# Issuing stores of token rows and routing weights, and the first loads of v, from other DMA queues

## The chip, the cores and the metric

The kernel runs on one core of a Trainium2 chip. Its engines are TensorE (PE, with its weight loads PEld), VectorE (DVE), ScalarE (ACT), GpSimd (POOL) and SyncE (SP). A DMA is started by an instruction in the queue of SP, ACT or POOL; the data are then moved by the core's 16 DMA engines. The metric is the device time of one execution in microseconds, as the median of several runs.

## The reference

Three layers follow each other on 4 x 576 = 2304 tokens of 512 values:

```python
scores = scale * q @ k.T + alibi_bias        # 4 batches, 8 heads, causal, window 128
x = softmax(scores) @ v                      # rows of 8 heads x 64
x = (silu(x @ w_gate) * (x @ w_val)) @ w_out # 512 -> 1536 -> 512
logits = x @ g_w + log1p(exp(x @ n_w)) * noise
out[token] = sum over its top 2 of 8 experts: weight * relu(x @ w1[e]) @ w2[e]
```

## The kernel before, in words

**Attention.** Heads go in pairs: a batch b has four pairs p. `load_qk` and `load_v` (lines 178 and 183) load a pair's q, k and v through `load_nat` (line 120), which starts three DMAs per tensor: one for each head's first 512 rows (line 124, 128 KB each) and one for the last 64 rows of both heads (line 125, 32 KB). Line 122 picks the queue: k of the very first pair goes by ACT, v of batch 0's first two pairs by POOL, all else by SP. At the start of the program the calls stand in this order (lines 191 to 195): q and k of pair 0, q and k of pair 1, v of pair 0, v of pair 1. The q, k and v of pairs 2 and 3 are loaded when an earlier pair has freed the buffer (line 535).

**First dense layer.** Its weights come in pieces of 512 KB. In batch group 0 each piece is loaded raw into `cs` by SP (`Convert.load`, line 221), rearranged by ACT (lines 246 and 247) and DVE (248 and 249) into `wst`, stored to a scratch tensor (line 250), and split into a high and a low part, `wu`, by ACT (line 295) and DVE (line 296). For later groups SP loads the scratch pieces into `wst` (line 279, three buffers) and ACT and POOL do the split. Each matmul is done as three (`three`, lines 321 to 323). The attention of group b+1 is interleaved with the dense layer of group b.

**Rows.** At the end of each group, `yo` (line 625) copies finished rows of 128 tokens from the accumulators to `X2` (tile xT), by ACT (line 644) or DVE (line 642), and stores each 128 x 512 block into the DRAM tensor `x2d` (line 646, POOL, 18 stores of 256 KB in all). A row of `x2d` has 520 values: 512 of the token, 8 routing weights.

**Routing and experts.** `route` is called twice, for the first three groups (13 blocks of tokens) and for the last one (5 blocks). Its `weigh` (line 770) computes the weights `wd` on ACT and DVE and stores them into the last 8 columns of `x2d` (line 782, POOL, two stores). From the chosen slots `decode` makes index lists, and `gather` (line 904) has POOL fetch expert rows from `x2d` by an indirect DMA. The expert weights w1, w2 pass through the same `wst` buffers (line 279, SP) and the same split.

**Order of work.** SP, ACT and POOL each work through one queue in order, DMA instructions included. Which instruction comes when is written by hand for DVE and POOL in the first stretch (to line 1007) and for PE in one stretch near the end (line 1063); elsewhere a scheduler orders each queue when the program is built, by playing the program through a timing simulation (`schedule_with_timeline_sim=True`, line 1164).

Of the kernel before, what the change touches and what calls it, by code (L numbers as in the profile page):

```python
# [24 lines left out]
def f32(ap):  # L25
    return ap.bitcast(F32)
# [3 lines left out]
def tile_alibi_window_attention__swiglu__noisy_top2_moe(  # L30
# [15 lines left out]
    nc = tc.nc  # L46
    B, H, S, D = q.shape
    DM = H * D
# [13 lines left out]
    TP = 128  # L62
# [6 lines left out]
    RW = DM + E  # L69
# [8 lines left out]
    def bank(i):  # L78
        return psum.tile([128, 512], F32, name=f"b{i}", tag=f"b{i}")

    x2d = dram.tile([NT, RW], F32, name="x2d")
# [37 lines left out]

    def load_nat(t, src, b, p, rest=None):  # L120

        eng = nc.scalar if src is k and (b, p) == (0, 0) else nc.gpsimd if src is v and b == 0 and p < 2 else nc.sync
        for i in range(2):
            eng.dma_start(t[:, 0:4, i, :], src[b, 2 * p + i, 0:512, :].rearrange("(i p) d -> p i d", p=128))
        eng.dma_start(t[0:64, 4] if rest is None else rest, src[b, 2 * p:2 * p + 2, 512:576, :].rearrange("h p d -> p h d"))
        return t
# [51 lines left out]
    def load_qk(b, p):  # L178
        qn, kn = (buffers(b, p).nat(x) for x in ("qn", "kn"))
        NAT[b, p, "q"] = load_nat(qn, q, b, p)  # L180
        NAT[b, p, "k"] = load_nat(kn, k, b, p, qn[64:128, 4])

    def load_v(b, p):
        bf = buffers(b, p)
        NAT[b, p, "i"] = bf.nv % 2
        bf.nv += 1
        load_nat(bf.v[NAT[b, p, "i"]], v, b, p)
# [131 lines left out]
    def three(ps, st, mv, first, last):  # L319

        nc.tensor.matmul(ps, st(0), mv(0), start=first, stop=False, skip_group_check=True)  # L321
        nc.tensor.matmul(ps, st(0), mv(1), start=False, stop=False, skip_group_check=True)  # L322
        nc.tensor.matmul(ps, st(1), mv(0), start=False, stop=last, skip_group_check=True)  # L323
# [4 lines left out]
    def new_xt(i, dt=F32R):  # L328
        return main.tile([128, 2, KC * GW], dt, name=f"xT{i % 2}")
# [4 lines left out]
    def xt_part(b, s):  # L334
        return XT[b][:, s, :].rearrange("p (c s) -> p c s", c=KC)

    def blocks(b):
        return GRP[b][1] // 128
# [235 lines left out]
    def gbank(b):  # L574
        gcount[0] += 1
        l = (0, 1, 2) if b < B - 1 else (0, 1, 2, 4, 5)
        return bank(l[gcount[0] % len(l)])

    def mlp1(b):

        base = b * UB
        n = GRP[b][1]
        cut = (0, n) if n <= 512 else (0, n // 2, n)

        def hh(s, f, sl):
            t, f = (HT[0], f) if f < NFA else (HT[1], f - NFA)
            return t[:, s, f * GW + sl.start:f * GW + sl.stop]

        def gv(f):
            st = {}  # L590

            def go(which, half, cs):
                def run():
                    u = base + 2 * f + which
                    sl = slice(cut[half], cut[half + 1])
                    w_ = sl.stop - sl.start
                    if cs.start == 0:
                        if half == 0:
                            ws.split(u + 3)
                        st["ps", which, half] = gbank(b)  # L600
                    w, ps = ws.tile[u], st["ps", which, half]
                    for c in range(cs.start, cs.stop):
                        three(ps[:, :w_], lambda s: w[:, s, c * 128:(c + 1) * 128],
                              lambda s: xt_part(b, s)[:, c, sl], c == 0, c == KC - 1)
                    if cs.stop < KC:
                        return
                    if which == 0:
                        t = wpool[1].tile([128, HW], F32, name="sg", bufs=3)[:, :w_]
                        nc.scalar.activation(t, ps[:, :w_], AF.Tanh, scale=0.5)
                        nc.vector.scalar_tensor_tensor(t, t, 1.0, ps[:, :w_], op0=OP.add, op1=OP.mult)  # L610
                        st["t", half] = t
                    else:
                        t = st["t", half]
                        nc.vector.scalar_tensor_tensor(t, t, 0.5, ps[:, :w_], op0=OP.mult, op1=OP.mult)
                        nc.scalar.activation(hh(0, f, sl), t, AF.Copy)  # L615
                        nc.vector.tensor_sub(hh(1, f, sl), t, f32(hh(0, f, sl)))  # L616
                return run
            parts = [slice(0, KC)] if len(cut) > 2 else [slice(0, 2), slice(2, KC)]
            return [go(w, h, cs) for w in range(2) for h in range(len(cut) - 1) for cs in parts]

        hidden = []
        for f in range(NF):
            hidden += gv(f)

        def yo(f, half):
            def run():
                u = base + 2 * NF + f
                if half == 0:
                    ws.split(u + 3)
                w = ws.tile[u]  # L630
                if f == 0 and half == 0:
                    std.l = dict(std.yo[blocks(b)])
                    YB1[b] = [bank(i) for i in range(blocks(b))]
                for i in range(2) if half == 0 else range(2, blocks(b)):
                    ps = YB1[b][i]
                    three(ps, lambda s: hh(s, f, slice(i * 128, (i + 1) * 128)), lambda s: w[:, s, :], f == 0, f == NF - 1)
                    if f == NF - 1:
                        if i == 0:
                            X2[b] = new_xt(b, F32)
                        o = X2[b][:, 0, i * DM:(i + 1) * DM]  # L640
                        if i % 2:
                            nc.vector.tensor_copy(o, ps)
                        else:
                            nc.scalar.activation(o, ps, AF.Copy)
                        r0 = GRP[b][0] + i * 128
                        nc.gpsimd.dma_start(x2d[r0:r0 + 128, 0:DM], o)
                if f == NF - 1 and half:
                    std.l = dict(std.gv)
            return run

        return hidden, [yo(f, h) for f in range(NF) for h in range(2)]
# [86 lines left out]
    def route(t0, t1, rt, early):  # L738
# [31 lines left out]
        def weigh():  # L770
            m, oh, sc = st["m"], st["oh"], st["sc"]
            w = [T("w0"), T("w1")]
            nc.vector.tensor_sub(m[1], m[1], m[0])
            nc.scalar.activation(w[1], m[1], AF.Exp)
            nc.vector.tensor_scalar(w[0], w[1], 1.0, 1e-9, op0=OP.add, op1=OP.add)
            nc.vector.reciprocal(w[0], w[0])
            nc.vector.tensor_tensor(w[1], w[1], w[0], op=OP.mult)
            wd = T("wd", E)
            nc.vector.tensor_tensor(wd, oh[0], bc(w[0]), op=OP.mult)
            nc.vector.tensor_tensor(sc, oh[1], bc(w[1]), op=OP.mult)  # L780
            nc.vector.tensor_tensor(wd, wd, sc, op=OP.add)
            nc.gpsimd.dma_start(x2d[t0 * TP:t1 * TP, DM:RW].rearrange("(t p) e -> p t e", p=TP), wd)
            msk = st["msk"] = T("msk", E, dt=BF)
            nc.vector.tensor_tensor(msk, oh[0], oh[1], op=OP.add)

# [70 lines left out]
        def done():  # L856
# [7 lines left out]
            decode(rt, early)  # L864

        return [noisy, pick(0), pick(1), weigh, slots] + [onehot(range(t, min(t + 2, nt))) for t in range(0, nt, 2)] + [done]

    def decode(rt, early):
# [157 lines left out]
    b = B - 1  # L1026
# [73 lines left out]
    with tc.If(n_over > 0):  # L1100
        with tc.tile_pool(name="ov", bufs=1) as ov:
            for e in range(E):
# [5 lines left out]
                with tc.For_i(CAP, n_e) as j:  # L1108
# [7 lines left out]
                    p = ov.tile([128, DM], F32, name="op")  # L1116
                    nc.gpsimd.indirect_dma_start(out=p, out_offset=None, in_=out,
                                                 in_offset=bass.IndirectOffsetOnAxis(ap=gi, axis=0))
                    t = bank(0)
# [49 lines left out]
```

## Time and profile before

| what | value |
|---|---|
| median of 3 runs | 1102.68 us (1100.41 to 1102.86) |
| the profiled execution | 1101.32 us, of which its span is 1099.5 us |
| PE / PEld busy | 1066.5 us (97%) / 917.8 us (83%) |
| DVE / ACT / POOL busy | 562.8 us (51%) / 461.3 us (42%) / 336.7 us (31%) |
| moved by DMA | 143.90 MB, mean 131 GB/s |
| mean granted PE clock | 0.99 |

The span runs from the first to the last profiled instruction; the time of the run has 1.82 us more around it. The profiled execution lies 1.36 us under the median of the runs. Shares of busy time are averages over stages, so the table says which engine is full, and the views by stretch of time say where it is not.

### The profile page before, as it was taken

What the parts mean: (1) busy time and instruction counts of PE and PEld (TensorE: products, weight loads), DVE (VectorE), ACT (ScalarE), POOL (GpSimd) and SP (SyncE); (2) the same over time, 40 slices, a digit from 0 to 9 for tenths busy, and PEclk for the clock granted to TensorE, in tenths of its full rate; (3) what the DMA queues carried; (4) which work ended last, traced back from release to release, by engine and by line L of the source; (5) the groups of instructions that cost most, each with busy time, mean ns of one, the idle gap of its engine ahead of it and who ended that gap; (6) DMA issues with size and microseconds to landing.
All of it is one profiled execution on the core that took longest, in us unless ns stands there. A gap on an engine that the chain in (4) does not pass through costs nothing.

```text
span 1099.5 us, 18123 instructions
## 1 busy us (share of the span) xinstructions
PE 1066.5 (97%) x6998; PEld 917.8 (83%) x6998; DVE 562.8 (51%) x1231; ACT 461.3 (42%) x1017; POOL 336.7 (31%) x344
## 2 busy tenths in 40 slices
PE   6889999999999999999999999999999999999995
PEld 5667778889988777779998888989898898989894
DVE  6778963577630477326885355535353434343320
ACT  6877854455532355434533233424232423232210
POOL 7200003122234333242378324414141414141301
PEclk9899999999999999999999999999999999999998
DMA  9688755332373233241322505636253535353201
GB/s 207 181 247 265 249 164 166 92 83 79 91 241 118 88 94 104 62 150 40 117 78 96 173 21 181 207 93 193 96 186 103 182 99 183 98 165 103 86 20 35
DMA packets 122064, 143.90 MB, mean 131 GB/s; under 512 B 63758, under 2 KB 92462, under 8 KB 121968
## 3 DMA queue, kind: packets, MB, share of 16 engines
q1 hardware_dynamic: 110064, 108.29, 32.4%
q0 software_dynamic: 10704, 34.06, 9.5%
q8 instruction: 57, 0.93, 0.3%
q10 hardware_dynamic: 1200, 0.30, 0.1%
q14 instruction: 39, 0.32, 0.1%
HBM read 113.84 MB, written 28.91 MB: 130 GB/s over the span
## 4 chain that ended last, share of the span: by engine, by line
PE 93%; DMA 2%; ACT 2%; DVE 1%; POOL 0%; issue 0%; SPq 0%; ACTq 0%; POOLq 0%; DVEq 0%
PE b L321 21%; PE b L322 20%; PE b L323 20%; PE b L935 19%; PE b L516 3%; PE b L486 2%; PE b L469 2%; PE b L919 1%; PE b L384 1%; DMA cs<-in_moe_w_val_dram 1%; PE b L704 1%; PE b L717 1%; DMA qn<-in_q_dram 0%; DMA xo<-x2d,gib 0%; ACT cs L247 0%; DMA kn<-in_k_dram 0%
## 5 line engine op out<-in xcount | busy, mean ns | idle before, releaser
L935 PE MATMUL b<-xT,wu 128*128 128x304 f32 (+2 forms) x1536 | 221.4, 303 | 0.0
L935 PEld LDWEIGHTS b<-xT,wu 128*128 128x128 f32 x1536 | 216.4, 188 | 2.2 <-DVE xT L923 0.3
L296 POOL TENSOR_TENSOR wu<-wst,wu 128x1024 fp32r<-128x1024 f32 x54 | 129.7, 2404 | 247.6 <-ACT wu L295 223.0
L321 PE MATMUL b<-xT,wu 128*128 128x320 f32 (+1 forms) x576 | 199.8, 351 | 4.6 <-ACT xT L531 4.5
L322 PE MATMUL b<-xT,wu 128*128 128x320 f32 (+1 forms) x576 | 197.7, 343 | 0.1
L323 PE MATMUL b<-xT,wu 128*128 128x320 f32 (+1 forms) x576 | 196.7, 342 | 0.0
L321 PE MATMUL b<-wu,hTa 128*128 128x512 f32 (+1 forms) x482 | 191.6, 400 | 0.0
L322 PE MATMUL b<-wu,hTa 128*128 128x512 f32 (+1 forms) x482 | 188.9, 392 | 0.0
L295 ACT ACTIVATE wu<-wst 128x1024 fp32r<-128x1024 f32 x136 | 143.6, 1058 | 105.1 <-PE b L323 79.6
L323 PE MATMUL b<-wu,hTa 128*128 128x512 f32 (+1 forms) x482 | 187.2, 392 | 0.0
L321 PEld LDWEIGHTS b<-xT,wu 128*128 128x128 f32 x576 | 107.8, 188 | 16.8 <-ACT xT L531 5.9
L296 DVE TENSOR_TENSOR wu<-wst,wu 128x1024 fp32r<-128x1024 f32 x82 | 100.3, 1224 | 39.5 <-ACT wu L295 39.4
L322 PEld LDWEIGHTS b<-xT,wu 128*128 128x128 f32 x576 | 109.3, 190 | 9.8 <-issue 1.6
L323 PEld LDWEIGHTS b<-xT,wu 128*128 128x128 f32 x576 | 109.0, 189 | 9.0 <-issue 1.5
L942 DVE SCALAR_TENSOR_TENSOR hTa<-b,hTa 128x304 fp32r<-128x304 f32 (+2 forms) x128 | 56.6, 469 | 114.5 <-ACT hTa L941 114.5
L941 ACT ACTIVATE hTa<-b 128x304 fp32r<-128x304 f32 (+2 forms) x128 | 50.4, 422 | 142.5 <-PE b L935 140.5
L323 PEld LDWEIGHTS b<-wu,hTa 128*128 128x128 f32 (+1 forms) x482 | 88.8, 184 | 21.0 <-issue 0.3
L321 PEld LDWEIGHTS b<-wu,hTa 128*128 128x128 f32 (+1 forms) x482 | 88.8, 184 | 19.0 <-issue 0.9
L322 PEld LDWEIGHTS b<-wu,hTa 128*128 128x128 f32 (+1 forms) x482 | 89.0, 185 | 18.6 <-issue 0.6
L912 POOL DMA_INDIRECT xo<-x2d,gib x37 | 36.3, 981 | 173.7 <-PE b L919 165.4
L922 ACT ACTIVATE xT<-b 128x512 fp32r<-128x512 f32 (+1 forms) x40 | 22.9, 574 | 142.1 <-PE b L919 142.1
L616 DVE TENSOR_TENSOR hTa<-sg,hTa 128x320 fp32r<-128x320 f32 (+1 forms) x54 | 69.1, 1285 | 23.0 <-ACT hTa L615 23.0
(199 smaller groups left out, 1298.9 us busy)
## 6 DMA issues: line engine op xcount, KB each, us to landing
wst<-in_moe_w_dram SPq DMA_DIRECT2D x64, 512.0 KB, 3.9
wst<-wscr SPq DMA_DIRECT2D x54, 512.0 KB, 3.3
wscr<-wst SPq DMA_DIRECT2D x18, 512.0 KB, 3.3
cs<-in_moe_w_gate_dram SPq DMA_DIRECT2D x12, 512.0 KB, 4.9
cs<-in_moe_w_val_dram SPq DMA_DIRECT2D x12, 512.0 KB, 6.3
cs<-in_moe_w_out_dram SPq DMA_DIRECT2D x12, 512.0 KB, 5.5
x2d<-xT POOLq DMA_DIRECT2D x18, 256.0 KB, 2.9
out_dram<-sg SPq DMA_DIRECT2D x1, 4608.0 KB, 16.0
```

Of the source, the lines that this page charges most:

```text
L295: nc.scalar.activation(o[0], s, AF.Copy)
L296: self.eng(n).tensor_sub(o[1], s, f32(o[0]))
L321: nc.tensor.matmul(ps, st(0), mv(0), start=first, stop=False, skip_group_check=True)
L322: nc.tensor.matmul(ps, st(0), mv(1), start=False, stop=False, skip_group_check=True)
L323: nc.tensor.matmul(ps, st(1), mv(0), start=False, stop=last, skip_group_check=True)
L516: mm.append(nc.tensor.matmul(x[64 * h:64 * h + 64, (j - j0) * 64:(j - j0 + w) * 64], wt, st["pt"][kk, h ^ sw, c:c + 64 * w], start=(n == 0 ...
L616: nc.vector.tensor_sub(hh(1, f, sl), t, f32(hh(0, f, sl)))
L912: nc.gpsimd.indirect_dma_start(out=x[0:r], out_offset=None, in_=x2d[0:GRP[-1][0], :] if (e, g) == (0, False) else x2d, in_offset=bass.Indi ...
L922: nc.scalar.activation(d[0], tv, AF.Copy)
L935: nc.tensor.matmul(ps[g][:, 0:hi - lo], w[:, a, c * 128:(c + 1) * 128], xgt(e, m, g)[:, c, 0:hi - lo], start=(c == 0 and a + m == 0), stop ...
L941: nc.scalar.activation(d, ps[g][:, 0:hi - lo], AF.Relu)
L942: nc.vector.scalar_tensor_tensor(h2[1][:, f, lo:hi], ps[g][:, 0:hi - lo], 0.0, f32(d), op0=OP.max, op1=OP.subtract)
```

## The change

Three lines change. In `load_nat` k and v of batch 0's pair 0 go by ACT's queue, and v of pair 1 goes by SP's. In `yo` the 18 stores of rows, and in `weigh` the two stores of routing weights, are issued by SP.

```diff
     def load_nat(t, src, b, p, rest=None):
-        eng = nc.scalar if src is k and (b, p) == (0, 0) else nc.gpsimd if src is v and b == 0 and p < 2 else nc.sync
+        eng = nc.scalar if src is not q and (b, p) == (0, 0) else nc.sync
...
-                        nc.gpsimd.dma_start(x2d[r0:r0 + 128, 0:DM], o)
+                        nc.sync.dma_start(x2d[r0:r0 + 128, 0:DM], o)
...
-            nc.gpsimd.dma_start(x2d[t0 * TP:t1 * TP, DM:RW].rearrange("(t p) e -> p t e", p=TP), wd)
+            nc.sync.dma_start(x2d[t0 * TP:t1 * TP, DM:RW].rearrange("(t p) e -> p t e", p=TP), wd)
```

## Rows read from the trace of the kernel before

**Rows 1.** The page: busy time by engine, share of the span, instructions.
```profile
PE 1066.5 (97%) x6998; PEld 917.8 (83%) x6998; DVE 562.8 (51%) x1231; ACT 461.3 (42%) x1017; POOL 336.7 (31%) x344
```

**Rows 2.** Busy time by stretch: PE, PEld, DVE, ACT, POOL, then clock, DMA share, GB/s.
```profile
0.00:20.00 20.00, 11.56 (x68) 9.50 (x69) 12.96 (x60) 10.94 (x38) 13.70 (x31) 1.00 0.89 189
20.00:40.00 20.00, 15.65 (x128) 12.03 (x126) 16.73 (x57) 17.42 (x52) 9.25 (x24) 0.83 0.95 264
40.00:80.00 40.00, 34.80 (x291) 26.88 (x290) 29.71 (x87) 30.51 (x76) 6.58 (x16) 0.91 0.75 210
80.00:130.00 50.00, 50.00 (x308) 38.66 (x306) 44.65 (x78) 39.27 (x70) 0.51 (x1) 1.00 0.74 239
```

**Rows 3.** The chain that ended last, its first part: start, duration, what.
```profile
1.26 4.01 DMA kn<-in_k_dram
...
9.54 5.32 DMA qn<-in_q_dram
14.87 0.57 SPq L124
...
18.73 11.37 DMA cs<-in_moe_w_val_dram
30.19 1.13 ACT wst L246
```

**Rows 4.** The timeline of the first 31 us: start, duration, engine, line; idle before in brackets.
```profile
1.84 0.69 ACTq L125 DMA_DIRECT2D qn<-in_k_dram  x1
3.93 1.28 ACT L393 ACT_TABLE_LOAD   x1 [3.93 <-DVE rc L108]
5.39 1.76 POOL L124 DMA_DIRECT2D v<-in_v_dram  x2
6.53 0.60 ACT L393 ACTIVATE kT<-b 128x512 f32<-128x512 f32 x1 [1.31 <-PE b L384]
6.66 1.07 SPq L124 DMA_DIRECT2D kn<-in_k_dram  x2
8.32 0.37 SPq L124 DMA_DIRECT2D hTb<-in_q_dram  x1
9.12 0.92 SPq L124 DMA_DIRECT2D qn<-in_q_dram  x2
12.09 0.52 POOL L410 COPY vz<-v 64x384 f32<-64x384 f32 x1
14.20 0.60 SPq L125 DMA_DIRECT2D hTb<-in_k_dram  x1
30.19 1.13 ACT L246 ACTIVATE wst<-cs 128x1024 f32<-128x1024 f32 x1 [0.70 <-DMA cs<-in_moe_w_val_dram]
```

**Rows 5.** Issues of line 124 on ACT: ns min/median/max, first and last start.
```profile
L124 ACTq DMA_DIRECT2D kn<-in_k_dram x2: 500/525/550, 0.7 to 1.3; - x2
```

**Rows 6.** Busy time around the lowered clock, columns as in rows 2.
```profile
30.00:32.50 2.50, 0.69 (x6) 0.42 (x4) 1.65 (x7) 2.31 (x3) 1.62 (x4) 0.98 0.64 144
32.50:35.00 2.50, 1.53 (x9) 0.96 (x9) 2.47 (x4) 2.16 (x5) 0.00 (x0) 0.50 0.85 255
35.00:37.50 2.50, 2.50 (x25) 2.16 (x25) 2.44 (x8) 1.76 (x5) 0.00 (x0) 0.50 1.03 349
```

**Rows 7.** Issues of the stores on POOL, lines 646 and 782, columns as before.
```profile
L646 POOL DMA_DIRECT2D x2d<-xT x18: 540/542/612, 184.1 to 629.9; - x18
L782 POOL DMA_DIRECT2D x2d<-wd x2: 872/1028/1183, 542.9 to 650.1; - x2
```

**Rows 8.** Waits of the engines: who for whom, us in total, times, longest.
```profile
POOL x2d L782 <- DVE wd L781: 25.2, 2, 19.7
...
POOL x2d L646 <- ACT xT L644: 12.6, 5, 8.7
...
ACT wu L295 <- DMA wst<-in_moe_w_dram: 10.9, 8, 1.8
```

**Rows 9.** The longest wait in SP's own queue, columns as in rows 8.
```profile
SPq L279 <- DVE wu L296: 320.4, 50, 22.7
```

## The prediction

> **What bounds the kernel now.** I read the busy times first, then the stretches, then the chain of waits inside the stretch that has room. PE is busy 1066.5 us of the span of 1099.5, so all other engines together can give back at most 33.0 us [rows 1]. The stretches show where these lie: PE is idle 8.44 us of the first 20, 4.35 us of the next 20 and 5.2 us from 40 to 80; from 80 to 130 it is full, and what is left is scattered and at the end [rows 2]. [...] So the six moved loads, all in the first 10 us, lie in the only place where something can be won or lost; the twenty moved stores come at 184 us or later, where PE is nearly full.
>
> The chain says what that early stretch waits for [rows 3]. The very first k lands at 5.27 us (1.26 + 4.01). Then SP is the thread: its issue at 14.87 comes 0.01 us after the landing of a q load whose flight began at 9.54 (9.54 + 5.32), and the last piece of raw weights issued at 18.73 lands at 30.11, where ACT had stood idle for 0.70 us [rows 3, 4]. From 20 to 40 the DMA engines are 0.95 busy and ACT 17.42 of 20 us [rows 2]: both are close to full, and ACT's wait for the weights is short. What comes later than now delays ACT at once; what comes earlier gains 0.70 us at most before ACT itself is the limit.
>
> **The change part by part.** The sum is made against the profiled execution, 1101.32 us, which is 1.36 under the median of 1102.68.
>
> *v of pair 0, from POOL to ACT.* POOL loses three issues, the first two 1.76 us together [rows 4], and does nothing new in the gap: what it next does with v is the copy at 12.09, which did not wait [rows 4]. Gain there: nothing. ACT gains two issues of 0.525 and one of 0.69, 1.74 us [rows 4, 5], behind its present last one, which ends at 2.53 (1.84 + 0.69). Back to back they end at 4.27. Its table load of 1.28 us, now released at 3.93, would then end at 5.55, and the first activation is released by PE at 6.53 [rows 4]: hidden, with 0.98 to spare. That is the lower bound, no cost. They need not go back to back. The issue at 14.87 came upon the landing of the one at 9.54, and between them SP issued eight DMAs, counted from that one to the one at 14.20 [rows 3, 4]; I read this as at most eight in flight over SP and ACT, an inference from one coincidence. Today six DMAs go out before 2.53 and POOL's do not count among them. If the third v load is about the twelfth, it waits for the fourth, which lands at 5.27 [rows 3]: it ends at 5.96, the table load at 7.24, and ACT starts 0.71 late. If all of pair 1's q and k stand before it, it waits for the seventh, issued at 2.53 and, at the 4.01 us that k took [rows 3], landed near 6.54: end 7.23, table 8.51, 2.0 us late. I take 0.7, since the two queues are ordered by the same simulated time and will alternate; bounds 0 and 2.0.
>
> *v of pair 1, from POOL to SP.* SP gets two more issues of 0.535 (half of 1.07) and one of 0.60, 1.67 us [rows 4], in front of the loads of pair 2 at 6.66. From there to 9.12 SP is idle twice, 7.73 to 8.32 and 8.69 to 9.12, 1.02 us in all [rows 4], since those loads wait for PE to free a buffer. So 0.65 us remains, and 1.67 if the idle moments move along. But the weights are not gated by issue alone: at 14.87 SP was let go by a landing, and the same bytes have to land in either kernel. Lower bound: POOL's traffic no longer mixes with SP's, the weights land earlier, and ACT's 0.70 us of idle time goes, a gain of 0.7. I take 0, between those, because it is nearest to the row at 14.87; bounds -0.7 and +1.67. The first part's 0.7 delays the same chain (the activation at 6.53 leads to the transpose that frees q's buffer for the load at 9.12), so the parts add: +0.7.
>
> [...]
>
> *The 18 stores of rows.* POOL saves 18 x 0.542 = 9.8 us and 12.6 us of waiting for copies [rows 7, 8], and the two weight stores save 2.1 us (0.872 + 1.183) and 25.2 of waiting [rows 7, 8]. POOL is busy 31% of the span and PE full, so I count no gain. What is late next: SP now stands in POOL's place and waits up to 8.7 us before a store of rows and up to 19.7 before one of weights, with loads for the dense layer or the experts queued behind. Its cover is the three buffers: SP spends 320.4 us in waits for the split to free one, and ACT's waits for an expert load are 10.9 us in eight [rows 8, 9]. The cost is 0 with this cover. Without it, each of the two longest waits could hold a load that ACT needs: at most 8.7 + 19.7 = 28 us late, of which PE would feel what exceeds its own stock of split weights. I take 0, because POOL's own waits in that place have left PE full.
>
> Sum: +0.7 on 1101.32, that is 1102.0 for an execution like the profiled one; with the 1.36 of the median, **1103.4 us**.
>
> **The rivals.** *Slower.* ACT's and SP's delays reach their upper ends together: 2.0 + 1.67 = 3.7 us. Place: ACT before its first activation, then the weight piece that lands at 30.11. It decides where ACT's third v load is issued after about 5.3 us and the piece lands after 31.8. For it: the DMA share of 0.95 and ACT's 17.42 leave nothing to catch up with [rows 2]; a longer gap of PE at 30 keeps the clock at 0.50 longer, and work now done in 5 us at that level shows the price, 0.5 us for each us of PE work. Against it: SP's idle moments. Time: 1102.68 + 3.7 + 0.5 x 1.5 (an estimate, for the extra work at the low level) = 1107.1.
>
> *Faster.* The loads come in another order, ACT's 0.70 us goes, and PE's gap at 30 closes, so that the clock stays up. The work of 1.53 and 2.50 us done at 0.50 [rows 6] would take half, 2.0 us less; 37.5 to 80, where the mean clock is also under 1, holds some more: from 40 to 80, 34.8 us of PE work at 0.91 is worth 3.1 us [rows 2]. Gain 0.7 + 2.0 + some 1.5 = 4.2: 1098.5. For it: since the schedule is made anew when the program is built, small shifts of loads can reorder ACT and PE here. Against: nothing in the change shortens ACT's own 17.42 us.
>
> *SP blocked by a store.* A weight store waits 5 to 20 us in SP's queue in front of a load with little slack; ACT's longest wait for a load is now 1.8 us [rows 8]. If a load were 5 us late and the stock covers 2, PE loses 3 us: 1105.7.
>
> *It moves nothing that matters.* All six loads are hidden, the stores as well: 1102.7. It gives the same verdict as the forecast.
>
> **How the numbers follow.** About 0.3%, 3.3 us, is what a measurement of this kernel can tell from no change. Forecast (+0.7) and "nothing" together 0.50, the slower rival 0.20, the blocked SP 0.05, the faster rival 0.25. Of the blocked case a little falls within 3.3 us and of the forecast's upper bounds a little outside; I leave it at faster 0.25, same 0.49, slower 0.26. The range goes from 1097.5 (the faster rival and 1 us more) to 1108.0 (the slower one and 0.9 more), leaving out cases in which a reordered schedule does far more. The forecast's own range is 1102.0 (-0.7) to 1106.4 (+3.7).
>
> **What the changed profile would show.** Right: in ACT's queue the third v load starts before 5.3 us and the first activation within 1 us of 6.53; the raw weights that landed at 30.11 land between 29.4 and 31.8; PE idle in the first 40 us stays near 12.8; stores appear on SP with no new line among ACT's or PE's waits, and POOL loses some 12 us of issues. Wrong: if ACT's first activation is 2 us late, the slower rival; if the low-clock stretch at 32.5 to 37.5 has gone or doubled, the clock decides and my terms were too small; if the waits of ACT for weight loads (now 10.9 us) grow to 20, SP's place in the stores; and if PE's order after 80 us differs, the scheduler moved more than this change names.

## The result: 0.84% slower, outside the range

The changed kernel takes 1111.49 us (median of 6 runs, 1109.43 to 1112.33), the kernel before 1101.98 in 6 runs beside it: a ratio of 1.0084, 95% interval 1.0072 to 1.0096. The forecast was 1103.4 and the range ended at 1108.0. The profiled execution of the changed kernel took 1112.33 us, the slowest of its six, with a span of 1110.5. One run of the kernel before, among the 24 beside the first four experiments, took 1310.98 us at a mean granted clock of 0.754 and is left out of all medians.

The page of the changed kernel, busy time by engine, beside [rows 1]:

```profile
PE 1069.8 (96%) x6998; PEld 920.3 (83%) x6998; DVE 564.5 (51%) x1231; ACT 461.3 (42%) x1017; POOL 320.1 (29%) x318
```

PE has 3.3 us more busy time in a span that is 11.0 longer: most of the loss is time in which PE does nothing. Busy time by stretch, the same four stretches as [rows 2]:

```profile
0.00:20.00 20.00, 11.91 (x61) 9.89 (x61) 11.42 (x49) 9.80 (x34) 8.02 (x21) 1.00 0.79 162
20.00:40.00 20.00, 14.31 (x121) 11.07 (x121) 15.79 (x64) 16.88 (x50) 9.43 (x27) 0.82 0.99 254
40.00:80.00 40.00, 34.81 (x287) 27.05 (x286) 28.82 (x88) 30.06 (x82) 7.84 (x17) 0.87 0.72 204
80.00:130.00 50.00, 50.00 (x292) 38.51 (x290) 44.56 (x77) 39.01 (x69) 1.03 (x1) 1.00 0.80 257
```

Up to 40 us PE is busy 1 us less, with 7 matmuls fewer in each of the first two stretches, and from 40 to 80 the mean clock is 0.87 instead of 0.91. The short stretches of [rows 6], in the changed kernel:

```profile
30.00:32.50 2.50, 1.26 (x20) 1.00 (x18) 2.20 (x7) 0.86 (x4) 0.04 (x1) 1.00 1.23 252
32.50:35.00 2.50, 0.23 (x3) 0.05 (x1) 0.45 (x1) 2.50 (x4) 1.58 (x4) 0.59 0.77 167
35.00:37.50 2.50, 1.90 (x10) 1.32 (x11) 2.47 (x5) 1.97 (x5) 0.00 (x0) 0.50 0.95 290
```

PE's gap has moved from the first of them to the second, where PE works 0.23 us, and the clock again goes to 0.50 with and after the gap; it stays there for 10.2 us (32.96 to 43.20), where it did for 6.8 before (32.42 to 39.25). The early part loses something, but not 11 us. The rest is at the other end. First the last instruction of DVE, from the timeline of each kernel (start, duration, engine, line), the kernel before and then the changed one:

```profile
1087.65 0.74 DVE L973 SCALAR_TENSOR_TENSOR hTb<-b,wcol,hTb 96x512 f32<-96x512 f32 x1 [4.77 <-PE b L323]
```

```profile
1093.02 0.75 DVE L973 SCALAR_TENSOR_TENSOR hTb<-b,wcol,hTb 96x512 f32<-96x512 f32 x1 [4.78 <-PEq L1100]
```

The computation ends 5.4 us later. From there to the end of the span it is 1099.5 - 1087.65 = 11.9 us before and 1110.5 - 1093.02 = 17.5 after: I call this the tail, and it is 5.6 us longer. In it POOL closes the program with two instructions, seen when one asks for lines 1100 and 1164 (engine, operation, count, ns min/median/max, first and last start). Before:

```profile
L1100 POOLq INC_SWDGE_SEM  x1: 1355/1355/1355, 1092.5 to 1092.5; - x1
...
L1164 POOLq DRAIN  x3: 46/103/4811, 1093.9 to 1099.2; - x3
```

After:

```profile
L1100 POOLq INC_SWDGE_SEM  x1: 2540/2540/2540, 1097.5 to 1097.5; - x1
...
L1164 POOLq DRAIN  x3: 46/107/9629, 1100.1 to 1110.3; - x3
```

INC_SWDGE_SEM takes 1.19 us more and the longest drain 4.82 more (6.0 together, of which 0.3 is made up on the way to them), and the last instructions of all other engines come after them. They belong to no line of the computation and are not counted as busy, so neither the busy times nor the costliest groups show them. Yet POOL issues 26 DMAs fewer than before.

### The profile page after: what moved, and what is told of

Read it like the earlier page. It is cut to its first block, busy times and chain, and to the rows that moved or that the text cites. A ratio compares the mean times of both kernels' runs of the same rounds, so it can differ in the third digit from the quotient of the medians.

```text
span 1110.5 us, 18117 instructions
## 1 busy us (share of the span) xinstructions
PE 1069.8 (96%) x6998; PEld 920.3 (83%) x6998; DVE 564.5 (51%) x1231; ACT 461.3 (42%) x1017; POOL 320.1 (29%) x318
## 5 line engine op out<-in xcount | busy, mean ns | idle before, releaser
L321 PEld LDWEIGHTS b<-xT,wu 128*128 128x128 f32 x576 | 108.0, 189 | 17.5 <-ACT xT L531 5.9
```

## The experiments

Each kernel is the kernel before with the edit shown, unless it says otherwise. The tail is read as above. **Pieces** counts the contiguous stretches of memory in the DMAs that are taken from POOL: 512 for a load of line 124, 128 for one of line 125, 128 for a store of rows, one per token for the weights. So the loads, the rows and the weights are 2304 pieces each. **Order** says whose order of instructions PE, DVE and ACT have, as their traces show it. **Rest** is the difference of the medians, against the runs of before on the same chip, less the difference of the tails, worked out before rounding. An interval of 0.001 to either side is 1.1 us, so a rest under about 1.5 us cannot be told from none; the tail and the last DVE instruction come from one profiled execution each.

| kernel | pieces off POOL | order | drain | tail | ratio, 95% interval | difference | rest |
|---|---|---|---|---|---|---|---|
| before | 0 | before | 4.81 | 11.9 | | | |
| after | 6912 | after | 9.63 | 17.5 | 1.0084 (1.0072 to 1.0096) | +9.5 | +3.9 |
| loads_only | 2304 | after | 3.42 | 9.9 | 1.0015 (1.0006 to 1.0025) | +2.4 | +4.4 |
| stores_only | 4608 | before | 1.87 | 8.0 | 0.9968 (0.9955 to 0.9981) | -3.3 | +0.6 |
| v0_act_only | 1152 | after | 4.08 | 10.7 | 1.0018 (1.0008 to 1.0028) | +2.4 | +3.5 |
| v1_sp_only | 1152 | a third | 4.08 | 10.7 | 1.0029 (1.0016 to 1.0042) | +4.2 | +5.4 |
| all_but_weights | 4608 | after | 1.87 | 8.1 | 0.9993 (0.9983 to 1.0003) | -0.4 | +3.4 |
| all_plus_filler | 4608 | after | 1.87 | 8.3 | 0.9994 (0.9985 to 1.0004) | -0.5 | +3.1 |
| before_plus_filler | -4608 | before | 7.59 | 15.3 | 1.0039 (1.0025 to 1.0053) | +4.8 | +1.4 |
| stores_and_v0 | 5760 | after | 1.22 | 7.4 | 0.9980 (0.9971 to 0.9990) | -1.7 | +2.8 |
| v0_act_tail_pool | 1024 | nearly after | 4.16 | 11.1 | 1.0032 (1.0021 to 1.0043) | +3.8 | +4.5 |
| v1_act_only | 1152 | after (PE, DVE) | 4.08 | 10.8 | 1.0035 (1.0023 to 1.0048) | +4.0 | +5.1 |
| v1_tail_sp | 128 | nearly before (PE) | 4.73 | 11.8 | 1.0003 (0.9994 to 1.0012) | +0.5 | +0.6 |
| swap_v_calls | 0 | a fourth | 4.81 | 11.6 | 0.9964 (0.9951 to 0.9977) | -3.8 | -3.6 |
| stores_and_swap | 4608 | the fourth | 1.87 | 8.0 | 0.9940 (0.9927 to 0.9954) | -6.3 | -2.4 |

**First, the parts alone.** The loads of v, all of them, with the stores left on POOL:

```diff
-        eng = nc.scalar if src is k and (b, p) == (0, 0) else nc.gpsimd if src is v and b == 0 and p < 2 else nc.sync
+        eng = nc.scalar if src is not q and (b, p) == (0, 0) else nc.sync
```

> Only line 122 is changed (v of pair 0 by ACT, v of pair 1 by SP); the stores stay on POOL. In the changed kernel the last DVE instruction starts 5.4 us later than before (1093.0 against 1087.7) and 5.6 us more follow it (17.5 us from there to the end of the span, against 11.9). Theory 1, the loads make the first part and the stores the second: the last DVE instruction near 1093.0, the stretch after it near 11.9, time near +5.4. Theory 2, the loads make both: near 1093.0 and 17.5, time near +10. Rival, the stores on SP hold up later loads and make the growth after 130 us: here the last DVE instruction comes near 1090.7 (+3.0), time near +3.

The 20 stores, with the loads left alone:

```diff
-                        nc.gpsimd.dma_start(x2d[r0:r0 + 128, 0:DM], o)
+                        nc.sync.dma_start(x2d[r0:r0 + 128, 0:DM], o)
...
-            nc.gpsimd.dma_start(x2d[t0 * TP:t1 * TP, DM:RW].rearrange("(t p) e -> p t e", p=TP), wd)
+            nc.sync.dma_start(x2d[t0 * TP:t1 * TP, DM:RW].rearrange("(t p) e -> p t e", p=TP), wd)
```

> Only lines 646 and 782 are changed (20 stores by SP); the loads stay as before. The order of instructions of PE, DVE and ACT is that of before. Theory 1: last DVE instruction near 1087.7, 17.5 us after it, time near +5.6. Theory 2: nothing, within 1 us of before. Rival (stores on SP hold up loads): the last DVE instruction 2 to 3 us later than before, and the delay first shows at one of the stores.

The loads of one pair only, with another line in place of the one removed above: v of pair 0 by ACT, and then v of pair 1 by SP.

```diff
+        eng = nc.scalar if src is not q and (b, p) == (0, 0) else nc.gpsimd if src is v and (b, p) == (0, 1) else nc.sync
```

> Only v of pair 0 moves, from POOL to ACT; v of pair 1 and the stores stay on POOL. PE, DVE and ACT have the order of instructions of the changed kernel. If the three issues in ACT's queue, with their waits, are what delays the first activation, and the order that follows from them, the delay of 2 us at 33 us and 4 to 5.4 us at the last DVE instruction is here in full. If SP's three more issues (v of pair 1) are what counts, the raw weights land near 30.1 as before and the delay at the end is under 2 us.

```diff
+        eng = nc.scalar if src is k and (b, p) == (0, 0) else nc.gpsimd if src is v and (b, p) == (0, 0) else nc.sync
```

> Only v of pair 1 moves, from POOL to SP; the rest as before. The order on PE, DVE and ACT is a third one. If SP's queue is what counts: raw weights land 1.5 to 2 us later than 30.1 and the time is +2 to +5. If ACT's queue is what counts: raw weights within 1 us of 30.1 and the time within 3 us of before, either way.

Neither theory held. The loads cost 2.4 us and the stores gain 3.3, which would make -0.9 together, and the whole is +9.5. The rival's figures for loads_only came true (its last DVE instruction starts at 1090.71), but not the rival: in stores_only that instruction starts at 1088.28, 0.6 us later than before and not 2 to 3. In v0_act_only the last DVE instruction comes 4.5 us later, at 1092.15, as its first case had it, though ACT begins with the raw weights only 1.24 later, at 31.43. v1_sp_only fits neither branch: ACT begins with the raw weights at 30.91, 0.72 later, and the time is 4.2 us longer all the same. Every part shortens the tail when it stands alone; only all of them together lengthen it. The stores in the queue of SP cost hardly anything; the waits in SP's queue in stores_only (who for whom, us in total, times, longest):

```profile
SPq L782 <- DVE wd L781: 22.2, 2, 17.3
...
SPq L646 <- ACT xT L644: 5.5, 9, 2.4
...
SPq L1164 <- PEq L1164: 1.9, 2, 1.3
```

SP does stand 17.3 us before a store of weights, as feared, but ACT's waits for weight pieces in the same kernel are what they were in [rows 8]:

```profile
ACT wu L295 <- DMA wst<-in_moe_w_dram: 10.7, 9, 1.7
```

**Second, what sets the tail.** Over the parts, the drain falls by 0.6 us for each 1000 pieces that leave POOL: 4.81, 4.08 (1152), 3.42 (2304), 1.87 (4608). At 6912 it is 9.63. A quantity that falls along a line and then jumps may go by a count that starts over; the ring of the expectations below is my guess at such a count. Two ways back from the changed kernel tell this apart from a cost of the moved stores. One is the changed kernel with the two weight stores back on POOL:

```diff
-            nc.sync.dma_start(x2d[t0 * TP:t1 * TP, DM:RW].rearrange("(t p) e -> p t e", p=TP), wd)
+            nc.gpsimd.dma_start(x2d[t0 * TP:t1 * TP, DM:RW].rearrange("(t p) e -> p t e", p=TP), wd)
```

> The changed kernel with the two stores of routing weights back on POOL; the row stores and the v loads stay moved, and the orders of PE, DVE and ACT are those of the changed kernel. Counted in contiguous pieces, each of the three edits takes 2304 pieces away from POOL (v loads 4 x 512 + 2 x 128, rows 18 x 128, weights 2304 x 1), so here 4608 are gone, as in stores_only. Ring theory (POOL's closing semaphore add and drain last as long as what POOL has issued since it last went round a fixed ring; 0.64 us less drain per 1000 pieces removed, and a jump up once between 4608 and 6912): add 0.64 us, drain 1.9 us, tail from the last DVE instruction to the end 8.0 us instead of 17.5, time 1102 us (9.5 less than the changed kernel). Rival (it is the stores of rows on SP together with the loads on SP, whatever the count): tail stays near 17.5 us, time 1111.

The other keeps the whole change and gives POOL more to do (`xw0` is a tensor like `x2d`):

```diff
-            nc.sync.dma_start(x2d[t0 * TP:t1 * TP, DM:RW].rearrange("(t p) e -> p t e", p=TP), wd)
+            nc.sync.dma_start(x2d[t0 * TP:t1 * TP, DM:RW].rearrange("(t p) e -> p t e", p=TP), wd); nc.gpsimd.dma_start(xw0[t0 * TP:t1 * TP, DM:RW].rearrange("(t p) e -> p t e", p=TP), wd)
```

> The changed kernel as it is, and beside it POOL stores the routing weights a second time, into a scratch tensor that nobody reads: 2304 pieces more on POOL, more work in all and nothing taken off SP or ACT; orders of PE, DVE, ACT and SP unchanged. Ring theory: as with all_but_weights, add 0.64, drain 1.9, tail 8.0 us, time 1102: a kernel with two more DMAs is 9 us faster. Rival (the tail comes with the moved stores): tail 17.5 or a little more, time 1111 to 1112.

Then the kernel before with two such stores behind line 782, into `xw0` and `xw1`:

```diff
-            nc.gpsimd.dma_start(x2d[t0 * TP:t1 * TP, DM:RW].rearrange("(t p) e -> p t e", p=TP), wd)
+            nc.gpsimd.dma_start(x2d[t0 * TP:t1 * TP, DM:RW].rearrange("(t p) e -> p t e", p=TP), wd); nc.gpsimd.dma_start(xw0[t0 * TP:t1 * TP, DM:RW].rearrange("(t p) e -> p t e", p=TP), wd); nc.gpsimd.dma_start(xw1[t0 * TP:t1 * TP, DM:RW].rearrange("(t p) e -> p t e", p=TP), wd)
```

> The kernel before, and POOL stores the routing weights two more times into scratch tensors: 4608 pieces more on POOL, orders of PE, DVE, ACT and SP unchanged. Ring theory: the line goes on the other way, add 1.35 + 0.71 = 2.06 us, drain 4.81 + 2.94 = 7.75 us, tail 11.9 + 3.65 = 15.5 us, time 1101.7 + 3.6 = 1105.3. Rival (the tail depends on the moves, not on the count): tail 11.9, time 1101.7, within 0.5.

And a count between 4608 and 6912, the edit of stores_only with the line of v0_act_only:

> All 20 stores on SP and only v of pair 0 on ACT (v of pair 1 stays on POOL): 5760 pieces gone, half way between stores_only (4608, drain 1.87 us) and the changed kernel (6912, drain 9.63 us); PE, DVE and ACT in the order of the changed kernel. Ring theory, jump after 5760: add 0.46, drain 1.14, tail near 7.2 us, last DVE instruction near 1092.5, time near 1101.5. Ring theory, jump before 5760: add 2.7, drain 10.4, tail 18.4, time near 1112.5. A tail in between, about 12.5 us, would speak against a jump.

In their tails all four came out near the ring theory's figures; of their times, before_plus_filler's is 1.3 us longer and stores_and_v0's 1.4 shorter than it said. The closing instructions of all_plus_filler:

```profile
L1100 POOLq INC_SWDGE_SEM  x1: 640/640/640, 1096.9 to 1096.9; - x1
...
L1164 POOLq DRAIN  x3: 46/107/1871, 1097.5 to 1100.0; - x3
```

The same two of before_plus_filler:

```profile
L1100 POOLq INC_SWDGE_SEM  x1: 2035/2035/2035, 1096.0 to 1096.0; - x1
...
L1164 POOLq DRAIN  x3: 46/103/7587, 1098.0 to 1106.2; - x3
```

And the drain of stores_and_v0:

```profile
L1164 POOLq DRAIN  x3: 46/103/1217, 1096.8 to 1098.6; - x3
```

Three kernels that differ in what POOL loads and stores but not in the count (stores_only, all_but_weights, all_plus_filler) have the same 640 and 1871 ns. Bytes do not decide it either: stores_only takes the weights, 72 KB, off POOL where all_but_weights takes the loads of v, 576 KB. The changed kernel with two more DMAs on POOL is 10 us faster than without (1101.23 against 1111.49; the runs of before beside them, 1101.76 and 1101.98, are alike). On the other side the line goes on: 2.035 and 7.59 us where 2.06 and 7.75 were expected. So the length of the closing drain goes by the number of pieces that POOL has issued, with one jump between 5760 and 6912 pieces fewer than before. That the jump is the wrap of a ring is my guess; no run shows a ring. The changed kernel is the only one in which POOL issues none of the 26 moved DMAs; two plain DMAs, the copies of a table at line 670, stay on POOL there too. What before_plus_filler loses beyond the tail, 1.4 us in the median and 3.5 in the profiled execution, is another matter, at the edge of what can be told. A likely part of it: the extra stores stand in POOL's queue ahead of the work for the index lists, and PE's waits there grow, from 1.0 and 0.4 us before. PE's waits in before_plus_filler:

```profile
PE b L853 <- DVE oa L847: 2.6, 3, 1.5
...
PE b L919 <- DMA xo<-x2d,gib: 1.2, 1, 1.2
```

In all_plus_filler, with one filler tensor instead of two, the first of these stayed at 1.0.

**Third, what the loads cost before the tail.** The column of the rest says it: 2.8 to 5.1 us in every kernel that has the order of the changed kernel, whether its loads go by ACT, by SP or both, and nothing measurable for the stores, which leave the order as it was. Moving the loads makes the scheduler lay the queues anew: in the trace 366 of PE's 6998 matmuls stand in other places than before, 292 of them after 80 us and the last at 174 us. Two theories were put against each other: it is the order, or it is the issues (ACT's late start, SP's longer queue). The first kernel takes away ACT's late start but keeps nearly that order:

```diff
+        eng = nc.scalar if src is not q and (b, p) == (0, 0) else nc.gpsimd if src is v and (b, p) == (0, 1) else nc.sync
...
-        eng.dma_start(t[0:64, 4] if rest is None else rest, src[b, 2 * p:2 * p + 2, 512:576, :].rearrange("h p d -> p h d"))
+        (nc.gpsimd if src is v and (b, p) == (0, 0) else eng).dma_start(t[0:64, 4] if rest is None else rest, src[b, 2 * p:2 * p + 2, 512:576, :].rearrange("h p d -> p h d"))
```

> Of v of pair 0 only the two big loads go by ACT; its small last one and v of pair 1 stay on POOL. ACT then has no third v issue that waits for the first landing of k: its first activation should start near 6.5 us as before, not 7.39. The order of DVE is that of the changed kernel, that of PE up to 9 lines. 1024 pieces leave POOL: tail about 11.1 us. Order theory (the loads cost what the new order of PE, DVE and ACT costs, not what the issues cost): the last DVE instruction 3 to 4.5 us later than before, as in v0_act_only, time 1104. Issue theory (ACT's late start and SP's longer queue are carried to the end): the 0.86 us and what follows from it go, last DVE within 0.7 of before, time 1101.

The second has exactly that order of PE and DVE with other issues, and the third nearly the order of before with a load moved:

```diff
+        eng = nc.scalar if src is k and (b, p) == (0, 0) or src is v and (b, p) == (0, 1) else nc.gpsimd if src is v and b == 0 and p < 2 else nc.sync
```

> v of pair 1 goes by ACT, v of pair 0 stays on POOL: three issues in ACT's queue as in v0_act_only, nothing more on SP. The orders of PE and DVE are exactly those of the changed kernel, SP's loads are nearly in before's order. 1152 pieces leave POOL: tail about 10.7 to 11. Order theory: last DVE 3 to 4.5 us later than before, time 1104, as in v0_act_only and loads_only. Issue theory: as late as ACT's first activation is (0.9 to 2 us), time near 1102.

```diff
+        (nc.sync if src is v and (b, p) == (0, 1) else eng).dma_start(t[0:64, 4] if rest is None else rest, src[b, 2 * p:2 * p + 2, 512:576, :].rearrange("h p d -> p h d"))
```

> Only the small last load of v of pair 1 (32 KB) goes by SP. The order of PE is that of before but for 7 lines; 128 pieces leave POOL, so the tail is as before, 11.8 us. Order theory: last DVE within 0.7 us of before, time 1101.7 within 0.7. Issue theory: SP's queue grows by 0.6 us ahead of the raw weights, and half of it or more arrives at the end: last DVE 0.3 to 0.6 later: the same within what can be told, so this run mainly tests that a nearly unchanged order costs nothing.

And one that moves no load to another queue, but has another order:

```diff
-    load_v(0, 0)
     load_v(0, 1)
+    load_v(0, 0)
```

> No queue is changed and POOL issues as many pieces as before; only the two calls that load v of pairs 0 and 1 change places, so POOL issues pair 1's v first. The scheduler then lays PE, DVE and ACT in another order than in any kernel so far (437 lines of difference to before in PE). Tail as before, 11.9 us. Order theory: last DVE 1 to 6 us later than before (or earlier, if before's order is no good one), time 1102.7 to 1107.7, though ACT and SP issue exactly what they did. Issue theory: v of pair 0 comes 1.9 us later on POOL than before and that is hidden, time 1101.7 within 0.7.

ACT's start in v0_act_tail_pool, from the timeline:

```profile
2.56 1.85 ACTq L124 DMA_DIRECT2D v<-in_v_dram  x2
4.50 1.28 ACT L393 ACT_TABLE_LOAD   x1 [4.50 <-DMA kn<-in_k_dram]
6.52 0.60 ACT L393 ACTIVATE kT<-b 128x512 f32<-128x512 f32 x1 [0.74 <-PE b L384]
```

ACT starts on time (6.53 in [rows 4]), and the kernel is as slow as the others: 1105.69 us. v1_act_only, with nothing more on SP, takes 1105.90, 2 us more than the order theory's 1104 and far from the issue theory's 1102. Neither takes all lateness away, though: SP's own order is new too, and the last early piece of raw weights, issued at 18.73 before [rows 3], is issued at 19.66 in the first and 20.18 in the second. v1_tail_sp, whose PE order differs from that of before in 7 lines (DVE's and ACT's differ in more), also issues that piece at 19.66 and is the same as before within what can be told; its last DVE instruction comes 1.8 us later, where 0.7 at most was expected, so that this one run taken alone speaks for neither. And swap_v_calls, in which no DMA changes its queue, comes out 3.8 us *faster*, with the tail of before; the order theory had left open to which side. ACT's work on that piece begins 1.06 us later there than before (30.19 in [rows 4]), so a late start on the weights does not decide the time. This start, and the last DVE instruction:

```profile
31.25 1.16 ACT L246 ACTIVATE wst<-cs 128x1024 f32<-128x1024 f32 x1
...
1086.47 0.75 DVE L973 SCALAR_TENSOR_TENSOR hTb<-b,wcol,hTb 96x512 f32<-96x512 f32 x1 [4.78 <-PE b L323]
```

The traces also show where the order costs, if one counts PE's matmuls between two points up to which both orders have done the same ones. The 512th starts at 85.6 us before and the 1100th, past the last difference in order, at 183.0. From the one to the other the eight kernels with the changed kernel's order, or nearly so, take 1.2 to 2.3 us longer than before, whatever their issues; stores_only, before_plus_filler and v1_tail_sp, with before's order or nearly so, are within 0.01 us of before. The two kernels with swapped calls gain 4.2 and 3.6 us from the 360th (59.8 us before) to the 1100th. Up to the 512th the eight are 0.6 to 3.6 us later than before, and v1_tail_sp 1.6; there order, late issues and the scatter of single executions cannot be told apart. Busy time from 80 to 185 us, before and then in the changed kernel, which gets through six matmuls fewer:

```profile
80.00:185.00 105.00, 105.00 (x628) 82.30 (x627) 73.81 (x136) 69.09 (x129) 6.53 (x6) 1.00 0.65 206
```

```profile
80.00:185.00 105.00, 104.52 (x622) 81.23 (x621) 76.74 (x138) 69.73 (x128) 3.93 (x3) 1.00 0.65 209
```

Orders laid by the scheduler thus go with rests from -3.6 to +5.4, 9 us apart, more than the 0.9 and 2.1 us by which issues came late in the changed kernel, and a kernel can gain by a new order without any DMA on another queue. What makes one order better than another was not settled. Busy time around the start, swap_v_calls, for the first 33 us and on to 80:

```profile
0.00:33.00 33.00, 23.95 (x143) 19.48 (x143) 21.90 (x95) 21.95 (x71) 20.45 (x50) 1.00 0.92 202
33.00:80.00 47.00, 40.87 (x329) 31.75 (x330) 34.95 (x88) 35.12 (x85) 11.79 (x21) 0.93 0.78 229
```

The changed kernel in the same stretches:

```profile
0.00:33.00 33.00, 21.78 (x147) 17.53 (x147) 21.86 (x97) 20.76 (x70) 16.37 (x45) 1.00 0.88 191
33.00:80.00 47.00, 39.25 (x320) 30.48 (x321) 34.17 (x102) 35.98 (x94) 8.92 (x20) 0.82 0.75 217
```

PE is busy 2.2 and 1.6 us longer in the good order, and the mean granted clock from 33 to 80 us is 0.93 against 0.82, so the clock is lowered less in that stretch. The clock alone does not rank the orders: it is 0.86 there in the kernel before, and 0.85 to 0.89 in the other kernels with the changed kernel's order. Which swap of neighbours begins this was not tried.

**Last, both at once.** The stores on SP and the swapped calls, without moving a load:

The edit is the two shown, of stores_only and swap_v_calls.

> The 20 stores on SP as in stores_only, and the two calls that load v of pairs 0 and 1 change places as in swap_v_calls; the v loads themselves stay on POOL. PE, DVE and ACT are in the order of swap_v_calls. If the two effects are independent, one in the order of the work and one in POOL's closing drain: last DVE near 1087.0 us (1086.5 of swap_v_calls and up to 0.6 for the stores), drain 1.87 and tail 8.0 us as in stores_only, span 1095, time 1095 (3.7 less than swap_v_calls' 1098.1 or a little less), so faster than both kernels. Rival: the gain of the swapped order is that profile's scatter of the clock, or SP's stores hold up loads in this order: last DVE 1088 or later, time 1097 to 1099.

The result is 1095.17 us (5 runs), 0.994 of before, faster than both kernels. Its last DVE instruction, from the timeline, and then its drain:

```profile
1085.71 0.75 DVE L973 SCALAR_TENSOR_TENSOR hTb<-b,wcol,hTb 96x512 f32<-96x512 f32 x1 [4.78 <-PE b L323]
```

```profile
L1164 POOLq DRAIN  x3: 46/103/1871, 1091.0 to 1093.4; - x3
```

The two effects add up as if independent, within the intervals: -3.3 and -3.8 make -7.1, and -6.3 was measured.

## Why the prediction was wrong

**v of pair 0 to ACT: right in size.** Forecast: the third v issue waits for a landing at 5.27, ACT starts 0.7 late. The changed kernel's timeline of ACT, and the raw weights' arrival at the end of the same stretch:

```profile
2.56 1.89 ACTq L124 DMA_DIRECT2D v<-in_v_dram  x2
5.30 0.60 ACTq L125 DMA_DIRECT2D v<-in_v_dram  x1
5.93 1.28 ACT L405 ACT_TABLE_LOAD   x1 [5.93 <-DMA kn<-in_k_dram]
7.39 0.59 ACT L405 ACTIVATE qT<-b 64x512 f32<-64x512 f32 x1 [0.17 <-PE b L384]
...
32.30 1.13 ACT L246 ACTIVATE wst<-cs 128x1024 f32<-128x1024 f32 x1 [1.64 <-DMA cs<-in_moe_w_val_dram]
```

The issue starts at 5.30 and the table load ends at 7.21, where 7.24 was forecast; the first activation, now another one than before, waits 0.17 more for PE and starts at 7.39, 0.86 late. The mechanism stands; what was wrong is that the 0.7 is not what the end is made of: v0_act_tail_pool has none of it and is no faster.

**v of pair 1 to SP: taken as 0; the weights left their window, but not by the added issues.** The weights were to be there between 29.4 and 31.8; ACT begins with them at 32.30 instead of 30.19, and waits 1.64 instead of 0.70 [rows 4]. SP's timeline in the changed kernel:

```profile
7.77 1.14 SPq L124 DMA_DIRECT2D xT<-in_v_dram  x2
8.96 0.60 SPq L125 DMA_DIRECT2D xT<-in_v_dram  x1
9.68 1.06 SPq L124 DMA_DIRECT2D qn<-in_q_dram  x2
...
20.78 0.51 SPq L221 DMA_DIRECT2D cs<-in_moe_w_val_dram  x1
```

The piece is issued at 20.78 instead of 18.73 [rows 3], 2.05 late, which looks like the 1.67 us of issue time and some more. Two other kernels say otherwise. The same issue in loads_only, with pair 1's v on SP, and then in v0_act_only, without it, there with the load of pair 2's k that stands in front:

```profile
20.40 0.51 SPq L221 DMA_DIRECT2D cs<-in_moe_w_val_dram  x1
```

```profile
10.88 1.14 SPq L124 DMA_DIRECT2D kn<-in_k_dram  x2
...
20.34 0.51 SPq L221 DMA_DIRECT2D cs<-in_moe_w_val_dram  x1
```

Nothing is added to SP in v0_act_only, and the piece is 1.61 late all the same; in these two executions the added issues make 0.06 us of difference, so SP's idle moments do take them up, as the 0 supposed. Most of the lateness is again an order laid anew, SP's own: k of pair 2, issued at 6.66 before [rows 4], where SP then stood idle, comes at 10.88 in v0_act_only, and its 1.14 us of issues stand behind SP's waits, in front of the weights. With the whole 1.67 us of added issue time in place of that 0 the sum would have been +2.4, and loads_only took just that, but by luck: 4.4 us of rest less 2.0 of tail.

**The failed step of this part** is that the loads were costed on a fixed order, and only in the first 80 us, "the only place where something can be won or lost": of the 5.4 us by which the computation ends later, 3.6 have arisen by PE's 512th matmul, 1.3 arise from there to its 1100th (85.6 to 183.0 us before), and 0.5 later. The text said that small shifts can reorder ACT and PE, but only as the rival on the faster side, with 4.2 us of gain; the slower rival got no reordering at all. The runs show it on both sides, with rests from -3.6 to +5.4 us. The criterion was named, that PE's order after 80 us would differ if the scheduler moved more than the change names, and it does differ; a chance and a price on the slower side were not given to it.

**The stores: the step that failed is "I count no gain" from POOL, taken as a term of 0.** SP's stores block nothing that matters: in the changed kernel too its longest wait before a store of weights is 17.3 us, and ACT's wait for weight pieces is 13.9 us, not the 20 of that rival. The waits of the changed kernel, first SP's and then ACT's:

```profile
SPq L782 <- DVE wd L781: 22.1, 2, 17.3
...
SPq L1164 <- PEq L1164: 9.6, 2, 9.1
SPq L646 <- ACT xT L644: 5.5, 9, 2.4
...
ACT wu L295 <- DMA wst<-in_moe_w_dram: 13.9, 9, 2.6
```

The line in between is the cost: 9.6 us in which SP waits for the end of the program, 4.8 before. What POOL saves was counted as nothing because POOL is idle most of the time; I never asked what POOL does after the last row of the computation. The trace of before had it: a span that ends 11.9 us after DVE's last instruction, with one POOL instruction of 4.8 us in it. That row alone shows neither the slope nor the jump, so the sign could not be worked out from it; but a term of some 5 us on the path, made by the engine whose DMAs the change takes away, belonged in the sum with bounds on both sides.

**The sum and the chances.** +0.7 was forecast and +9.5 measured: 5.6 in POOL's closing instructions, 3.9 before them, which comes with the new order; what the late issues of the first 85 us add to it was not separated. The slower rival's time, 1107.1, is near what the order alone makes (1101.98 + 3.9 = 1105.9), by another mechanism, which is luck. The range of 1097.5 to 1108.0 would have held that; it was the tail that went out of it.

## What to carry to other kernels

Look at the end of the span as one looks at its beginning: subtract the start of the last computing instruction from the span, and ask which instruction fills that time, since nothing busy may. When a queue is changed in a program whose order is laid by a scheduler, compare the built orders before explaining a time by the moved instructions; a swap of two lines can be worth more than the move. And parts tried alone need not add up: here -3.3 and +2.4 made +9.5, and only counts, not stories about queues, told why.

## What was not expected of the hardware

The closing drain of POOL falls by 0.62 us for each 1000 pieces taken from POOL's DMAs ((4.81 - 1.22) / 5.76) up to 5760 pieces, and at 6912 it is longer than at any other count. Carried on from 5760 to 6912 the line gives 0.50 us; the measured 9.63 lies 9.13 above it, and is twice the drain of the kernel before. Why it jumps between these two counts no run shows.

The limit of eight DMAs in flight over SP and ACT, inferred from one coincidence before, showed again, and it is the built program's. In the traces of the two kernels all DMAs of SP and ACT (314 before, 340 in the changed kernel) signal their landing through eight semaphores in turn (POOL's 143 and 117 use eight others), and an issue waits until the last user of its own has landed: the closest one starts 0.016 us after it. In the changed kernel the third v issue waits so for the second load of k, which lands at 5.28, and starts at 5.30; in v0_act_tail_pool, without that third issue, ACT starts on time.
